# Attention with two mixture-of-experts layers in one kernel: scores by weight part, pages one per block, wide idle products in the opening, another order in the drain

## The chip, the cores and the metric

One core of a Trainium2 chip runs the kernel, with its five engines: TensorE (PE), VectorE (DVE), ScalarE (ACT), GpSimd (POOL) and SyncE (SP). The metric is the time of one execution on the device in microseconds (us); lower is better.

## What is computed

The inputs are q, k and v of shape (2 batches, 8 heads, 576 rows, 64 columns) in f32. Each row of the scores keeps its 32 largest values, and a softmax over these weighs the rows of v. The result goes through two mixture-of-experts layers with 8 experts each.

```python
scores = scale * np.matmul(q, k.transpose(0, 1, 3, 2))
kth = np.partition(scores, -top_k, axis=-1)[..., -top_k:-top_k + 1]
scores = np.where(scores >= kth, scores, -1000000000.0)
attn = np.exp(scores - np.max(scores, axis=-1, keepdims=True))
attn = attn / (np.sum(attn, axis=-1, keepdims=True) + 1e-09)
x = np.matmul(attn, v)                       # then (2 * 576, 8 * 64)
x = _moe_ref(x, ...)                         # argmax expert, capacity, relu(x @ w1) @ w2, times the gate
return _moe2_ref(x, ...)                     # the same without a capacity
```

## The kernel before, in words

The attention stage cuts the work into 8 units (2 heads of one batch each) and every unit into 9 blocks of 128 query rows: 4 per head, and one, the fifth in order (tile `None`), that holds the last 64 rows of both heads and so needs twice the products (the two-head tile). That makes 72 blocks, numbered 0 to 71, and 36 pairs. `seq` gives their order. One pass of the loop `for i in range(L)` deals with several blocks at once, each at another step, and the order in which the program issues instructions is written out by hand there:

- `scores(*seq[i + 4])`: TensorE multiplies q and k, both split into a high and a low f32r part that lie below each other, in two weight parts (four for the two-head tile). Columns 0 to 511 go to a score bank `sc` (a bank of its own for each of the two blocks of a pair, two pairs in flight), the last 64 columns to the end of `pt`. ScalarE copies both into `s` (lines 319).
- `folds` and `chain` on VectorE find the 32nd largest value: `folds` takes maxima and minima of quarters of a pair of blocks ("hi", line 338, is its first instruction and reads `sc` and `s` of both blocks), and each block's `chain` is four MAX8 and three MATCH_REPLACE8. `woven` puts a pair's two chains and the folds of the next pair into one order, from a string of letters.
- `limits` (GpSimd) makes the bounds of a finished pair; `lowered` (GpSimd, `shifted`) and `below` (ScalarE, a relu, `under`) then prepare a block, and `flip` on TensorE transposes `shifted` into `pt` and adds the transposed `under` as a large negative number, so that `expo` (ScalarE, `pT`) gives zero for all that is not kept.
- `value` multiplies `pT` with v and with ones and gates beside it; `value_out` copies the sums out.

Each unit's q, k and v are transposed some blocks ahead through one page buffer `pg`: six pages `turn`, one `turn_tails`, one `v_turn` (line 294, emptied by ScalarE at line 295) and one `v_gates` (line 301, emptied at 302). The table that `at(i, job, ...)` fills says in which block each runs: `turn` in blocks i0-12 to i0-7 ahead of the unit's first block i0, `turn_tails` in i0-6, `v_turn` in i0-3, `v_gates` in i0-2. The last two share their blocks with the first two `turn` of the next unit.

`begin` does the first unit's transposes and the first four blocks' scores. `spin` issues products of a constant tile with zeros, whose results nobody reads; `free` is a piece of 74 columns of the bank `xb`.

The last four blocks are the drain, with an order of their own (`drain`, `back_half`). The last block's kept scores come from VectorE: `first_shift` and `first_exp` take the exponent of all scores with the row's maximum off, and one instruction into `kept` multiplies by "not below the 32nd". Behind that stand the check counts (`missed`, `flags`), the last sums, and the gating of the first mixture-of-experts layer (line 1200 on), which also frees the loads of its weights.

## Time and profile before

| | |
|---|---|
| three timed runs | 631.38, 629.01, 631.46 us; median 631.38 |
| profiled execution | 631.72 us, its span 630.1 us |
| mean granted TensorE clock | 0.96 of full speed |
| busy TensorE / VectorE / ScalarE / GpSimd | 598.6 / 502.4 / 417.5 / 192.0 us |
| attention stage | to about 286 us |

The span is what the trace covers; the time also has what lies around it. Times in rows count from the span's start. PE is TensorE's products, PEld its loading of weights, which runs beside them; a product's row is longer than its distance to the next, since products overlap. "<-" names whom an engine waited for. The granted clock is 1.00 at 2.4 GHz and 0.50 at 1.2 GHz.

### The profile page before, as it was taken

The numbers are of one execution on the slowest core, as the hardware profiler recorded it, in microseconds if no ns is written. First come the engines' busy times: TensorE is split into PE (matmuls) and PEld (weight loads), VectorE is DVE, ScalarE is ACT, GpSimd is POOL, SyncE is SP. The second block draws the span as 40 slices with busy tenths as digits, with TensorE's granted clock in tenths as the row PEclk, the third lists the DMA queues.
The fourth block names the chain that finished last, engine by engine and source line by source line (L and its number), as shares of the span: only waits on it lengthen the run. The fifth ranks groups of instructions, "written<-read, shape, count | busy, mean of one in ns | idle before, by whom it ended". The sixth has DMA issues, their size and how long they took to land.

```text
span 630.1 us, 13986 instructions
## 1 busy us (share of the span) xinstructions
PE 598.6 (95%) x4839; PEld 556.4 (88%) x4839; DVE 502.4 (80%) x1728; ACT 417.5 (66%) x970; POOL 192.0 (30%) x422
## 2 busy tenths in 40 slices
PE   8899999999999999896999999999999999999995
PEld 6788989898989899785889999999999899999984
DVE  6868999999999999967677788785358797888740
ACT  5467878786878787641477777775246578787641
POOL 8356355645465334324201011100011312111010
PEclk7589999998999999986899999999999999999999
DMA  7610150416070000004797677677394976777650
GB/s 147 156 40 20 45 151 21 126 29 128 21 137 2 20 2 20 1 20 138 265 354 234 207 241 218 220 270 260 110 301 169 339 250 230 234 270 259 219 204 19
DMA packets 78640, 96.05 MB, mean 152 GB/s; under 512 B 33797, under 2 KB 40453, under 8 KB 78560
## 3 DMA queue, kind: packets, MB, share of 16 engines
q1 hardware_dynamic: 73632, 84.07, 43.0%
q0 software_dynamic: 3728, 10.70, 5.2%
q8 instruction: 41, 0.67, 0.4%
q10 hardware_dynamic: 1200, 0.30, 0.2%
q14 instruction: 39, 0.32, 0.2%
HBM read 82.32 MB, written 13.22 MB: 152 GB/s over the span
## 4 chain that ended last, share of the span: by engine, by line
PE 38%; DMA 8%; issue 4%; DVE 1%; ACT 0%; POOLq 0%; POOL 0%; ACTq 0%; DVEq 0%
PE pp L1041 8%; DMA out_dram<-yr,sidx 8%; PE pp L1080 7%; PE pp L1043 3%; PE pp L1082 3%; PE pp L1034 2%; PE pt L998 2%; PE pl L1094 1%; PE pp L1038 1%; PE pp L1037 1%; PE pp L1074 1%; PE pp L1039 1%; PE pp L1078 1%; PE pp L1076 1%; PE pp L1077 1%
## 5 line engine op out<-in xcount | busy, mean ns | idle before, releaser
L412 PE MATMUL xb<-vx,pT 128*128 128x73 f32 (+1 forms) x800 | 95.2, 269 | 0.0
L1041 PE MATMUL pp<-xT,w1c 128*128 128x416 f32 (+4 forms) x320 | 93.9, 361 | 0.5 <-DVE xT L1004 0.5
L412 PEld LDWEIGHTS xb<-vx,pT 128*128 128x128 f32 (+1 forms) x800 | 88.3, 183 | 2.3 <-issue 1.6
L969 DVE TENSOR_TENSOR w2c<-raw,w2c 128x512 fp32r<-128x512 f32 x112 | 74.2, 686 | 17.9 <-ACT w2c L968 17.8
L1080 PE MATMUL pp<-hT,w2c 128*128 128x416 f32 (+4 forms) x320 | 88.0, 353 | 0.0
L1082 PE MATMUL pp<-hT,w2c 128*128 128x208 f32 (+4 forms) x320 | 78.5, 245 | 0.0
L1043 PE MATMUL pp<-xT,w1c 128*128 128x208 f32 (+4 forms) x320 | 77.9, 243 | 0.0
L391 PE MATMUL pt<-ident,shifted 128*128 128x128 f32 x355 | 70.1, 283 | 3.6 <-ACT pT L400 2.1
L968 ACT ACTIVATE w2c<-raw 128x512 fp32r<-128x512 f32 x112 | 66.7, 623 | 7.8 <-SPq L1336 4.1
L969 DVE TENSOR_TENSOR w1c<-raw,w1c 128x512 fp32r<-128x512 f32 x96 | 60.8, 687 | 7.7 <-ACT w1c L968 7.4
L392 PE MATMUL pt<-negid,under 128*128 128x128 bf16 x355 | 66.0, 223 | 0.0
L1020 ACT ACTIVATE t<-pp 128x208 f32<-128x208 f32 (+4 forms) x120 | 37.6, 313 | 41.2 <-PE pp L1043 29.6
L1041 PEld LDWEIGHTS pp<-xT,w1c 128*128 128x128 f32 x320 | 60.1, 188 | 1.5 <-DVE xT L1004 0.9
L1082 PEld LDWEIGHTS pp<-hT,w2c 128*128 128x128 f32 x320 | 61.2, 191 | 0.0
L1043 PEld LDWEIGHTS pp<-xT,w1c 128*128 128x128 f32 x320 | 61.1, 191 | 0.0
L391 PEld LDWEIGHTS pt<-ident,shifted 128*128 128x128 f32 x355 | 51.0, 144 | 10.9 <-POOL lg L437 2.2
L1080 PEld LDWEIGHTS pp<-hT,w2c 128*128 128x128 f32 x320 | 60.2, 188 | 0.0
L356 DVE MAX8 top<-y 128x8 f32<-128x160 f32 x216 | 58.7, 312 | 0.0
L968 ACT ACTIVATE w1c<-raw 128x512 fp32r<-128x512 f32 x96 | 53.5, 621 | 7.2 <-SPq L1336 6.1
L319 ACT ACTIVATE s<-sc 128x512 f32<-128x512 f32 x72 | 43.0, 598 | 19.5 <-PE sc L318 17.5
L382 ACT ACTIVATE under<-s,nb 128x576 bf16<-128x576 f32 x71 | 54.2, 766 | 2.3 <-POOL nb L374 2.3
L385 POOL TENSOR_SCALAR shifted<-s,nb 128x576 f32<-128x576 f32 x71 | 53.2, 752 | 5.7 <-PE pt L392 1.6
(327 smaller groups left out, 1441.7 us busy)
## 6 DMA issues: line engine op xcount, KB each, us to landing
raw<-in_moe_w_dram SPq DMA_DIRECT2D x62, 1024.0 KB, 5.8
out_dram<-zero SPq DMA_DIRECT2D x3, 768.0 KB, 3.7
y<-yr POOLq DMA_DIRECT2D x8, 256.5 KB, 4.4
kraw<-in_k_dram SPq DMA_DIRECT2D x8, 256.0 KB, 3.1
vraw<-in_v_dram SPq DMA_DIRECT2D x16, 128.0 KB, 3.0
vx<-in_v_dram SPq DMA_DIRECT2D x16, 128.0 KB, 2.6
w2c<-in_moe_w_dram SPq DMA_DIRECT2D x4, 512.0 KB, 7.5
x<-xn SPq DMA_DIRECT2D x15, 128.0 KB, 1.8
```

The lines of the kernel that those rows point to most:

```text
L356: ops.append(lambda w=w, cur=cur: nc.vector.max(w, cur))
L382: nc.scalar.activation(under[k % 3][:, :S], s, AF.Relu, bias=nb[:, 1:2], scale=-BIG)
L385: nc.gpsimd.tensor_scalar(shifted[k % 3][:, :S], s, nb[:, 0:1], 1.0, op0=OP.add, op1=OP.mult)
L391: both = (nc.tensor.matmul(pt[:, o], shifted[k % 3][:, o], ident, is_transpose=True, start=True, stop=False), nc.tensor.matmul(pt[:, o], u ...
L392: nc.tensor.matmul(pt[:, o], under[k % 3][:, o], negid, start=False, stop=True))
L412: nc.tensor.matmul(o, pT[:, c2, cols], z["v"][:, c2, hh], start=(c2 == 0), stop=(c2 == NC - 1))
L968: nc.scalar.activation(o[:, 0], src_, AF.Copy)
L969: nc.vector.tensor_tensor(o[:, 1], src_, o[:, 0].bitcast(F32), op=OP.subtract)
L1041: nc.tensor.matmul(ph[:, :2 * n].rearrange("p (w n) -> p w n", w=2), w[f][:, 0, d], xT[:, d, :, :n], start=st, stop=False)
L1043: nc.tensor.matmul(ph[:, :n], w[f][:, 1, d], xT[:, d, 0, :n], start=False, stop=sp)
L1080: nc.tensor.matmul(py[:, :2 * n].rearrange("p (w n) -> p w n", w=2), w[f][:, 0, o], hT[:, f, :, :n], start=st, stop=False)
L1082: nc.tensor.matmul(py[:, :n], w[f][:, 1, o], hT[:, f, 0, :n], start=False, stop=sp)
```

## The change

1. `scores` goes through the weight parts one by one, and with each through both pieces of columns; before it did one piece with all parts, then the other. The second block's products no longer depend on the copy of the first block's scores.
2. `v_turn` and `v_gates` of units 2 to 7 run in blocks i0-5 and i0-4; unit 1's stay in blocks 6 and 7.
3. In the opening `wide_spin` (512 columns, read as twice the same 256) takes the place of most `spin`, in fewer products; in `begin` they write to the second bank of pair 1.
4. The drain is written anew: the values of block 67 and the flip of 68 come earlier, the chain of block 68 runs ahead of that of 69, `limits` of that pair is done by halves, and both last blocks (70 and 71) get the exponent by `apart` and the product by `keep` on VectorE.

The rest of the loop issues what it issued before.

```diff
-            kept = wk.tile([128, NC * 128], F32, name="kept", bufs=1)
-            nc.gpsimd.memset(kept[:, S:], 0.0)
+            kept = [wk.tile([128, NC * 128], F32, name=f"kept{i}", bufs=1) for i in range(2)]
...
+                z_ = pair(k_)
+                sc, s = z_.sc, z_.s
+                places_ = ((pt_[:, M * 128:S], slice(M * 128, S)), (sc[:, j_], slice(0, M * 128)))
+                for n_, (l, r) in enumerate(ops):
+                    for w_, (o, w) in enumerate(places_):
+                        m_ = nc.tensor.matmul(o, l, r[:, w], start=(n_ == 0), stop=(n_ == len(ops) - 1))
+                        if w_ and j_ and z_.read is not None:
+                            tc.declare_no_dep(m_.ins, z_.read.ins, reason="two banks")
+                for w_, (o, w) in enumerate(places_):
                     a_ = nc.scalar.activation(s[:, j_, w], o, AF.Copy)
...
+            def wide_spin(n, o):
+                for _ in range(n):
+                    nc.tensor.matmul(o.rearrange("p (a b) -> p a b", a=2), ones,
+                                     idle[:, None, :].to_broadcast([128, 2, 256]), start=True, stop=True)
...
-                spin(5, free)
+                pair(0)
+                wide_spin(2, pair(1).sc[:, 1])
...
-                spin(4, free)
+                wide_spin(3, pair(1).sc[:, 1])
...
-                spin(12, free)
+                wide_spin(4, pair(1).sc[:, 1])
...
-                    at(i0 - 3, v_turn, u)
-                    at(i0 - 2, v_gates, u)
+                    at(6 if u == 1 else i0 - 5, v_turn, u)
+                    at(7 if u == 1 else i0 - 4, v_gates, u)
...
-                if i < 5:
+                if i < 4:
+                    wide_spin((6, 6, 6, 3)[i], xb)
+                elif i == 4:
                     spin(12, free)
...
+            rest = bank()
+            a, b = chain(L - 4), chain(L - 3)
+            vec = woven((a, b), folds(K - 1, (0, 1)), "fafafafafbabafbabfabffb")
+            limits(K - 3)
+            relus = [fresh(L - 6), fresh(L - 5)]
+            run_jobs(L - 4, False)
+            do(vec[:17])
+            back(L - 7, lambda: do(relus))
+            back(L - 6)
+            run_jobs(L - 4, True)
+            run_jobs(L - 3, False)
+            do(vec[17:])
+            back(L - 5)
+            limits(K - 2, slice(0, 1))
+            relu = fresh(L - 4)
+            relu()
+            wide_spin(3, rest[:, 0])
+            value(L - 5)
+            value_out(L - 5)
+            pTs[L - 4] = expo(flip(L - 4))
+            run_jobs(L - 3, True)
+            limits(K - 2, slice(1, 2))
+            relu = fresh(L - 3)
+            run_jobs(L - 2, False)
+            a, b = chain(L - 2), chain(L - 1)
+            vec = woven((a, b), [], "ab" * 7)
+            do(vec[:2])
+            relu()
+            es = [apart(L - 2), apart(L - 1)]
+            do(vec[2:13])
+            keep(L - 2, es[0])
+            do(vec[13:])
+            keep(L - 1, es[1])
+            wide_spin(2, rest[:, 0])
+            back(L - 3)
...
+            wide_spin(2, rest[:, 0])
             value(L - 3)
             value_out(L - 3)
...
-            pTs[L - 2] = expo(flip(L - 2))
+            for c in range(NC):
+                o = slice(c * 128, c * 128 + 128)
+                nc.tensor.transpose(pt_[:, o], kept[0][:, o], ident)
+            pT = pTs[L - 2] = wk.tile([128, NC, 128], F32, name="pT")
+            nc.scalar.activation(pT.rearrange("p c s -> p (c s)"), pt_, AF.Copy)
```

Where instructions now stand, at three places. TensorE in the opening, behind the first unit's first three pages: of the small idle products the first is shown (`xb<-identr` are the tails' transposes, 64 columns). Before:

```order
L254 MATMUL sc<-identr,ks 128x128 x3
L479 LDWEIGHTS ones
L479 MATMUL xb<-idle,ones 128x74
...
L254 MATMUL xb<-identr,qs 128x64 [waits DVE_49]
L254 MATMUL xb<-identr,ks 128x64
```

And now:

```order
L255 MATMUL sc<-identr,ks 128x128 x3
L494 LDWEIGHTS ones
L494 MATMUL sc<-idle,ones 128x512 [waits Activation_49]
...
L255 MATMUL xb<-identr,qs 128x64 [waits DVE_49]
L255 MATMUL xb<-identr,ks 128x64
```

The wide products go to a score bank, and the first of them has a wait for ScalarE that the small ones had not.

TensorE in the blocks ahead of a unit (unit 2; `pg<-ident,vraw` is `v_turn`, `pg<-wgh` is `v_gates`, `pg<-identr` is `turn` of the unit after it). Before, in block i0-3:

```order
L412 MATMUL xb<-vx_144,pT 128x73 x5
L294 MATMUL pg<-ident,vraw 128x128 [waits DMAHW6_49,DMAHW5_49,PE_49]
L294 MATMUL pg<-ident,vraw 128x128 x3
L254 MATMUL pg<-identr,qs 128x128 [waits Activation_49]
L254 MATMUL pg<-identr,qs 128x128 x3
```

Now, in block i0-5:

```order
L423 MATMUL xb<-vx_146,pT 128x73 x4
L295 MATMUL pg<-ident,vraw 128x128 [waits DMAHW6_49,DMAHW5_49,PE_49]
L295 MATMUL pg<-ident,vraw 128x128 x3
L319 MATMUL pt<-qkT 128x64 [waits Activation_49]
L319 MATMUL sc<-qkT 128x512 [waits DVE_49]
```

The v page is followed by scores in place of another page, and the page behind it no longer waits for ScalarE at that point.

ScalarE in the drain (`pT` are exponents, `xl` the sums copied out, `under` the relus, `e` the exponents for the kept blocks). Before, from the exponents of blocks 66 and 67 on:

```order
L400 ACTIVATE pT<-pt 128x640 [waits PE_49,Activation_49] x2
L425 ACTIVATE xl_124<-xb 128x146 [waits PE_49]
L382 ACTIVATE under_139<-s,nb 128x576 [waits Pool_49]
L382 ACTIVATE under_131<-s,nb 128x576
L666 ACTIVATE e<-s,nb_4213 128x576 [waits Pool_49]
L400 ACTIVATE pT<-pt 128x640 [waits PE_49,Activation_49]
L425 ACTIVATE xl_124<-xb 64x146 [waits PE_49]
```

And now:

```order
L411 ACTIVATE pT<-pt 128x640 [waits PE_49,Activation_49] x2
L436 ACTIVATE xl_124<-xb 128x146 [waits PE_49]
L393 ACTIVATE under_141<-s,nb 128x576 [waits Pool_49]
L436 ACTIVATE xl_124<-xb 64x146 [waits PE_49]
L411 ACTIVATE pT<-pt 128x640 [waits PE_49,Activation_49]
L393 ACTIVATE under_133<-s,nb 128x576 [waits Pool_49]
L679 ACTIVATE e<-s,nb_4202 128x576 [waits Pool_49]
L679 ACTIVATE e<-s,nb_4206 128x576 [waits Pool_49]
```

The relu of block 69 (`under` behind the last `pT`) now stands behind the sums of block 67 and the exponent of 68, and both `e` stand behind that relu.

## Rows read from the trace of the kernel before

**Rows 1.** Busy time by stretches: length; each engine's busy us (x instructions); TensorE clock; DMA; GB/s.

```profile
9.20:9.50 0.30, 0.14 (x2) 0.02 (x1) 0.15 (x1) 0.30 (x1) 0.30 (x1) 0.80 0.62 46
10.00:20.00 10.00, 9.21 (x45) 7.61 (x45) 8.02 (x32) 4.31 (x13) 6.18 (x16) 0.50 0.65 149
36.00:38.00 2.00, 2.00 (x23) 1.82 (x21) 2.00 (x8) 1.28 (x5) 1.92 (x5) 0.83 0.00 0
60.00:80.00 20.00, 19.84 (x175) 18.06 (x174) 20.00 (x88) 16.74 (x38) 8.34 (x20) 1.00 0.19 60
272.00:274.00 2.00, 1.98 (x13) 1.48 (x14) 2.00 (x13) 1.54 (x3) 1.93 (x5) 0.55 0.23 65
```

**Rows 2.** Who waited for whom: VectorE in 0 to 170 us, TensorE in 62 to 262.

```profile
DVE hi L338 <- ACT s L319: 13.8, 11, 2.8
...
PE pg L254 <- ACT vT L295: 3.4, 5, 0.7
PE pg L254 <- ACT vx L302: 1.7, 5, 0.3
```

**Rows 3.** Timeline of VectorE, its "hi" instructions: start, length, in brackets the wait before.

```profile
18.07 0.46 DVE L338 TENSOR_TENSOR hi<-sc,s 128x288 f32<-128x288 f32 x1 [0.60 <-ACT s L319]
...
24.66 0.46 DVE L338 TENSOR_TENSOR hi<-sc,s 128x288 f32<-128x288 f32 x1 [1.44 <-ACT s L319]
...
34.38 0.46 DVE L338 TENSOR_TENSOR hi<-sc,s 128x288 f32<-128x288 f32 x1 [2.79 <-ACT s L319]
...
43.42 0.46 DVE L338 TENSOR_TENSOR hi<-sc,s 128x288 f32<-128x288 f32 x1 [2.10 <-ACT s L319]
...
59.57 0.46 DVE L338 TENSOR_TENSOR hi<-sc,s 128x288 f32<-128x288 f32 x1 [1.91 <-ACT s L319]
...
94.39 0.46 DVE L338 TENSOR_TENSOR hi<-sc,s 128x288 f32<-128x288 f32 x1 [0.29 <-ACT s L319]
...
123.10 0.46 DVE L338 TENSOR_TENSOR hi<-sc,s 128x288 f32<-128x288 f32 x1 [1.20 <-ACT s L319]
...
159.46 0.46 DVE L338 TENSOR_TENSOR hi<-sc,s 128x288 f32<-128x288 f32 x1 [1.36 <-ACT s L319]
```

**Rows 4.** Timeline of the opening: idle products on TensorE, and ScalarE's reading of the pages.

```profile
1.33 3.79 PE L479 MATMUL xb<-idle,ones 128*128 128x256 bf16 x17 [1.33 <-DVE idle L68]
...
6.27 1.05 ACT L504 ACTIVATE qkT<-sc 128x512 fp32r<-128x512 f32 x2
...
12.96 0.79 PEld L479 LDWEIGHTS <-ones 128*128 128x128 bf16 x12
12.96 0.96 PE L479 MATMUL xb<-idle,ones 128*128 128x74 bf16 x12
...
41.14 0.58 PE L479 MATMUL xb<-idle,ones 128*128 128x74 bf16 x12
```

**Rows 5.** Timeline of TensorE in the two blocks with two pages each, before unit 3.

```profile
112.27 0.55 PE L254 MATMUL pg<-identr,qs 128*128 128x128 f32 x4 [0.69 <-ACT vT L295]
...
116.96 0.54 PE L254 MATMUL pg<-identr,ks 128*128 128x128 f32 x4 [0.34 <-ACT vx L302]
```

**Rows 6.** Timeline of the drain: TensorE, ScalarE, VectorE, and the gating's first instruction.

```profile
269.29 1.29 PE L412 MATMUL xb<-vx,pT 128*128 128x73 f32 x10
...
272.02 0.34 PE L391 MATMUL pt<-ident,shifted 128*128 128x128 f32 x1 [1.45 <-POOL shifted L385]
...
272.73 0.78 ACT L666 ACTIVATE e<-s,nb 128x576 f32<-128x576 f32 x1
...
273.67 2.40 PE L412 MATMUL xb<-vx,pT 128*64 128x73 f32 x20
...
274.74 0.83 DVE L708 SCALAR_TENSOR_TENSOR kept<-s,top,e 128x576 f32<-128x576 f32 x1
...
282.21 2.35 PE L412 MATMUL xb<-vx,pT 128*128 128x73 f32 x20
...
285.81 0.24 DVE L1200 TENSOR_REDUCE mx<-lg 128x10 f32<-128x80 f32 x1 [0.33 <-DVEq L766]
```

## Prediction: what the change does to the time

> **What bounds the kernel now.** I read the page first, then busy time by stretches, then the waits, then the timeline of one VectorE instruction, and last the queues at the places that the edits touch. The profiled execution took 631.72 us over a span of 630.1, and the timed runs have a median of 631.38: a sum made against 631.72 stands 0.3 us above the median. All edits lie in the attention stage, which ends with the gating that starts at 285.81 us [rows 6]; the 344 us of mixture-of-experts stages behind it are not edited, and start when the gating is done.
>
> Between 60 and 80 us VectorE is busy for 20.00 of 20 us and TensorE for 19.84 [rows 1]: two engines side by side at their limit. VectorE's work on a pair of blocks begins with the instruction on "hi", so the starts of these are the clock of the stage. Where nothing is late they lie 6.8 to 7.0 us apart. What is late stands in brackets [rows 3], and it is always ScalarE's copy of the scores. In the first 170 us VectorE waits for that copy 13.8 us, 11 times [rows 2]. The change works at three places.
>
> First, the opening. The granted TensorE clock falls at 9.4 us, is 0.50 for the whole of 10 to 20 us, and comes back between 36 and 38 us [rows 1]. On that level TensorE's work takes longer: twelve small idle products 0.96 us against 0.58 at full clock [rows 4]. The waits at 18.07, 24.66 and 34.38 us, 0.60 + 1.44 + 2.79 = 4.83 us, lie in that stretch; those at 43.42 (2.10) and 59.57 (1.91) lie behind it, at full clock [rows 3].
>
> Second, the middle. From 62 to 262 us TensorE waits 3.4 + 1.7 us for ScalarE to empty the one page buffer [rows 2]. That happens where two pages stand in one block: the v page is followed at once by a q page, which waits 0.69 us, and in the next block the v gates by a k page, which waits 0.34 [rows 5]. These are the third and second block before a new unit, just ahead of the scores of the two-head tile, which have eight products where others have four. There VectorE waits 1.20 us at 123.10 and 0.29 at 94.39 [rows 3]; each of the two comes once more later, as the units alternate.
>
> Third, the drain. TensorE stands idle 1.45 us before 272.02, for the shifted block, and works from there to the last two values, which end at 284.56 (282.21 + 2.35) [rows 6], at first with a clock of 0.55 [rows 1].
>
> **The change part by part.** *Wide idle products.* The 5 + 4 + 12 small products around the first scores become 2 + 3 + 4 of 512 columns; the 12 in each of the first four blocks become 6, 6, 6 and 3. By the 17 products of 256 columns at the start, 3.79 us or 0.22 each [rows 4], a wide one takes 0.44 us at the low clock, and half, 0.22, at the full one (estimates). Against: the first two now go to the bank of pair 1, whose page ScalarE reads until 7.32 us (6.27 + 1.05) [rows 4]; the small ones ran at 6.4 us. The tails' transposes and all first scores are queued behind them and move back by 0.85 us. For: ahead of the fall at 9.4 us TensorE had transposes, small products and waits; now 5 wide products, 1.1 us of dense streaming, stand there, and 1.3 us more in each of the first blocks. I take it that the clock stays up through most of the opening. Then the three waits in the low stretch go, 4.83 us, less 0.85 for the late start: **-4.0 us**. Followed forward along ScalarE's copies, the "hi" of 24.66 comes at 22.5 (VectorE then no longer waits), that of 34.38 at 29.8 and that of 43.42 at 38.4, where most of its wait is left, which would be 4.6 to 5.0. I keep the lower number, since near 25 us TensorE still has a gap with eight transposes and a wait for ScalarE. Bounds: with the clock as low as before, 30 wide ones take 13.2 us for 5.5 (69 small ones at 0.08), 7.7 more, less 1.0 for a wait of the first pairs that the third edit removes: +6.7; at best -5.0.
>
> *Pages one per block.* For units 2 to 7 the v page moves from 3 to 5, and the v gates from 2 to 4 blocks before the unit, where no other page stands. Nothing is added: the same transposes, gate products and copies, no DMA, past no queue but TensorE's and ScalarE's own. The two waits, 0.69 + 0.34 = 1.03 us per unit, go [rows 5]. The scores of the two-head tile come 1.03 us earlier, which takes 1.03 of each 1.20 and all of each 0.29 [rows 3]: 2 x (1.03 + 0.29) = **-2.6 us**. Unit 1 keeps its places, so the wait at 59.57 stays. The 1.36 us at 159.46 [rows 3] follow a low-clock stretch, and I leave them. Bounds: 0, if TensorE is late at the two earlier blocks instead; -4.0 with these 1.36.
>
> *Scores by weight part.* The same products, and a dependency less: the second block of a pair no longer waits for the copy of the first. In the steady part I put nothing down: TensorE's instructions stay as many. VectorE hides them where it is the bound; where it waits they cost what they cost now. The Trainium skill, "TensorE: Matmul & The Clock Gate", section "Step-by-step: what each phase is for", says that weights may be loaded once and used by many products, which would save half the loads now that two products with the same weights stand together. The trace disagrees: twelve idle products with the same ones bring twelve loads [rows 4]. By the page's rule the rest of the two-head waits (0.3) and the 1.91 at 59.57 could go, and the sum would be 2.2 us lower.
>
> *The drain.* I follow TensorE's queue. The values of block 66 (of 0 to 71) end at 270.4 in both (269.29 + 1.1) [rows 6]. Then three wide products, 0.65, which fill the idle time of now; the twenty value products of block 67 at full clock, 2.2, to 273.25 (they stand behind the wait and the low clock now: from 273.67 on); the flip of block 68, 0.85 (1.65 from 272.02 to 273.67 at the low clock, half at the full one) to 274.1. Its exponent and the relu of block 69 follow on ScalarE, 0.7 to 0.8 each like "e" [rows 6], to 275.5. That is late next: the relu is queued behind both, and the flip of 69 waits for it. Flip 0.9, values 1.1, two wide 0.45, values 1.1: 279.05. The two exponents of the last pair are queued behind that relu and end near 277; VectorE's last chain stands still some 1.9 us for the first, and the two kept products, 0.83 each [rows 6], end at 278.2, before TensorE asks for them. Ten transposes 1.05, flags and two wide 0.5, the last values 2.35: 282.95 in place of 284.56, **-1.6 us**. VectorE's count and GpSimd's gate sums, which end with it now, move up as much. Removed are a shift on GpSimd, a relu, a flip; added a kept product, an exponent, five transposes. Bounds: 0, if the wait for the exponents holds up VectorE's flags and count; -2.8, if the relu is not late.
>
> Sum: 631.72 - 4.0 - 2.6 - 1.6 = **623.5 us**. About 0.5% (3.2 us) is what a measurement of this kernel can tell from no change.
>
> **The rivals.** *A, the clock drops within the opening.* For it: near 25 us TensorE has transposes and a wait, as before the fall at 9.4. A low stretch as at 272 [rows 1] lengthens six wide products by 1.3 and a pair of scores by 0.5, and the "hi" at 29.8 becomes 31.5; a second one doubles that. Opening -1.0: 626.5 us. The Trainium skill, the same page, section "Part 4: PE-mode transpose", says that transposes do not count as busy for the clock gate; by that rule A is likelier, as mostly transposes stand between the wide products. No row here separates the two. Against: the wide products follow in each of these blocks. Chance 0.25.
>
> *B, the clock rises no earlier than now.* Then the wide products are work at half speed on the engine that VectorE waits for: +6.7, and -4.2 from pages and drain: 634.2 us, slower than before. It is decided by the end of the first six wide ones, near 24 us: if the clock is 0.50 there, this is the case. For it: 20 us of scores and transposes at 0.50 [rows 1] did not bring the clock up. Against: they never streamed 2.6 us in one piece, as six wide ones do. Chance 0.10.
>
> *C, pages and drain give little.* VectorE and TensorE are both full [rows 1]: what the two-head tile gains can be lost at the blocks that now carry the pages, and in the drain the exponents behind the relu can delay flags and count; or the stage behind, whose start lies at a low clock, takes a part back. The opening's 4.0 and 0.6 of the rest: 627.1 us. Chance 0.15.
>
> **How the numbers follow.** Forecast 0.50 (623.5, own range 620 to 626), A 0.25, C 0.15, B 0.10. The best bounds together, -5.0 - 4.0 - 2.8, give 619.9, and the gating's own low clock can move all by 1 to 2 us. The range reaches to A and C and leaves B out: 618 to 630. Faster by over 0.5% (under 628.2) are nearly all of the forecast, three quarters of A, two thirds of C: 0.78. Within 0.5%, the rest of these and half of B: 0.15. Slower 0.07.
>
> **What would show it.** Right: a clock of 1.00 from 10 to 30 us; the "hi" of 34.38 near 30; brackets under 0.3 at the two-head pairs; TensorE's page waits near zero; a gating that starts near 277.5. Wrong: 0.50 still at 24 us, brackets above 2 us before 40, a 1.20 left in the middle, or a TensorE that waits for the kept blocks.

## The result, and the profile after

The changed kernel takes 622.72 us (median of four runs, 621.69 to 623.75), the kernel before 631.42 in the same comparison (629.01 to 634.45): a ratio of 0.986, interval 0.9814 to 0.9905, or 8.7 us less. The forecast was 623.5. The profiled execution took 622.74 us over a span of 621.1, at a mean clock of 0.98 (before: span 630.1, 0.96).

The total came out nearly as forecast, its parts did not. In the changed kernel "hi" is line 348, the scores line 319, the flip 402, the values 423, wide idle products 494. Four stretches make the span: to the ninth "hi", which ends the opening; from there to the last "hi"; from the last "hi" to the gating; and the stages behind.

| us | before | after | change | forecast |
|---|---|---|---|---|
| ninth hi starts | 66.43 | 61.61 | -4.82 | -4.0 |
| ninth to last hi (264.19, 253.50) | 197.76 | 191.89 | -5.87 | -2.6 |
| last hi to gating (285.81, 275.91) | 21.62 | 22.41 | +0.79 | -1.6 |
| gating to the span's end | 344.29 | 345.19 | +0.90 | 0 |

**The opening.** First the stretches of after, with the columns of [rows 1]; the stretches 9.20 and 10.00 stand there for before.

```profile
9.20:9.50 0.30, 0.30 (x2) 0.10 (x1) 0.07 (x1) 0.21 (x2) 0.23 (x1) 1.00 0.27 23
10.00:20.00 10.00, 9.10 (x55) 6.11 (x54) 9.26 (x37) 6.39 (x17) 6.29 (x15) 1.00 0.67 156
26.00:28.00 2.00, 2.00 (x9) 0.78 (x7) 2.00 (x11) 0.60 (x1) 0.42 (x3) 0.54 0.72 162
28.00:30.00 2.00, 2.00 (x11) 1.61 (x10) 0.72 (x4) 0.44 (x2) 1.23 (x4) 0.60 0.71 160
254.00:256.00 2.00, 0.25 (x2) 0.22 (x3) 2.00 (x8) 1.78 (x4) 1.84 (x5) 0.72 0.00 0
256.00:258.00 2.00, 2.00 (x13) 1.75 (x12) 2.00 (x11) 0.32 (x1) 0.82 (x3) 0.50 0.20 56
260.00:262.00 2.00, 2.00 (x15) 1.74 (x12) 1.97 (x12) 0.57 (x1) 1.31 (x3) 0.58 0.00 0
292.00:299.00 7.00, 6.57 (x36) 6.27 (x37) 3.63 (x8) 2.46 (x5) 0.94 (x1) 0.53 1.04 348
```

The clock no longer falls at 9.4 us; 10 to 20 us run at 1.00. A short low stretch (granted clock at 0.50) stands at 26 to 29.5, a long one in the drain (254.5 to 262), a short one behind the gating (282 to 285.5), and one over the first expert's products (292 to 299). The "hi" instructions of after, as in [rows 3]:

```profile
11.03 0.31 DVE L348 TENSOR_TENSOR hi<-sc,s 128x144 f32<-128x144 f32 x1 [0.23 <-ACT s L323]
...
16.75 0.44 DVE L348 TENSOR_TENSOR hi<-sc,s 128x288 f32<-128x288 f32 x1
21.80 0.44 DVE L348 TENSOR_TENSOR hi<-sc,s 128x288 f32<-128x288 f32 x1
30.41 0.46 DVE L348 TENSOR_TENSOR hi<-sc,s 128x288 f32<-128x288 f32 x1 [1.70 <-ACT s L323]
38.62 0.46 DVE L348 TENSOR_TENSOR hi<-sc,s 128x288 f32<-128x288 f32 x1 [1.27 <-ACT s L323]
...
54.76 0.46 DVE L348 TENSOR_TENSOR hi<-sc,s 128x288 f32<-128x288 f32 x1 [1.92 <-ACT s L323]
61.61 0.44 DVE L348 TENSOR_TENSOR hi<-sc,s 128x288 f32<-128x288 f32 x1
...
116.42 0.45 DVE L348 TENSOR_TENSOR hi<-sc,s 128x288 f32<-128x288 f32 x1
...
253.50 0.40 DVE L348 TENSOR_TENSOR hi<-sc,s 128x288 f32<-128x288 f32 x1
```

**The middle.** No bracket is left between 61.61 and 253.50. Of TensorE's waits in 62 to 252 us those for the page [rows 2] are gone, and one for the exponents has come, which costs nothing: VectorE is busy for 190.00 of these 190 us.

```profile
PE pt L319 <- ACT pT L411: 2.8, 5, 1.0
```

**The drain.** Its rows in the timeline of after (start, length, in brackets the wait), to set beside [rows 6]:

```profile
255.75 0.45 PE L402 MATMUL pt<-ident,shifted 128*128 128x128 f32 x1 [2.37 <-POOL lg L448]
...
262.52 0.81 PE L494 MATMUL sc<-idle,ones 128*128 128x512 bf16 x3
...
267.11 1.43 ACT L679 ACTIVATE e<-s,nb 128x576 f32<-128x576 f32 x2
...
267.91 0.82 DVE L684 SCALAR_TENSOR_TENSOR kept<-s,top,e 128x576 f32<-128x576 f32 x1 [4.05 <-ACT e L679]
...
275.91 0.24 DVE L1251 TENSOR_REDUCE mx<-lg 128x10 f32<-128x80 f32 x1 [0.33 <-POOL lg L791]
```

TensorE stands idle 2.37 us before the flip of block 66, as it did before the change (2.13 us, then without a fall):

```profile
266.42 0.30 PE L391 MATMUL pt<-ident,shifted 128*128 128x128 f32 x1 [2.13 <-ACT pT L400]
```

This time the clock falls there. Two flips and two sets of values, 255.75 to 262.52, take 6.77 us; all behind them is late, and VectorE waits 4.05 us for an exponent.

**Behind the gating.** The first expert's products begin in these rows, the upper one before the change, the lower one after it:

```profile
304.29 0.35 PE L1037 MATMUL pp<-xT,w1c 128*128 128x256 f32 x1 [0.19 <-issue]
```

```profile
291.95 0.35 PE L1088 MATMUL pp<-xT,w1c 128*128 128x256 f32 x1 [1.45 <-issue]
```

That is 18.48 and 16.04 us behind the gating, 2.4 us gained; from there to the span's end it is 325.81 and 329.15 us, 3.3 lost. In the changed kernel the clock is low from 292 to 299 us, over these products; before the change it was back by 303 us, ahead of them. How much of the 3.3 us this low stretch takes is not shown: after_again (below) has none there and still needs 327.65 us for that part.

### The profile page after: what moved, and what is told of

It is laid out like the page before. It is cut to its first block, busy times and chain, and to the rows that moved or that the text cites. A ratio compares the mean times of both kernels' runs of the same rounds, so it can differ in the third digit from the quotient of the medians.

```text
span 621.1 us, 13886 instructions
## 1 busy us (share of the span) xinstructions
PE 592.1 (95%) x4789; PEld 548.1 (88%) x4789; DVE 501.8 (81%) x1729; ACT 417.4 (67%) x970; POOL 191.5 (31%) x423
## 4 chain that ended last, share of the span: by engine, by line
PE 37%; DMA 8%; issue 5%; DVE 2%; ACT 1%; POOLq 0%; POOL 0%; ACTq 0%; DVEq 0%
DMA out_dram<-yr,sidx 8%; PE pp L1092 8%; PE pp L1131 7%; PE pp L1094 3%; PE pp L1133 3%; PE pp L1085 2%; PE pl L1145 1%; PE pp L1089 1%; PE pp L1088 1%; PE pt L1049 1%; PE pp L1090 1%; PE pp L1125 1%; PE pp L1127 1%; PE pp L1129 1%; PE pp L1128 1%
## 5 line engine op out<-in xcount | busy, mean ns | idle before, releaser
L402 PE MATMUL pt<-ident,shifted 128*128 128x128 f32 x350 | 68.5, 281 | 2.9 <-POOL lg L448 2.4
L403 PE MATMUL pt<-negid,under 128*128 128x128 bf16 x350 | 64.5, 222 | 0.3 <-ACT under L393 0.3
L319 PE MATMUL sc<-qkT 128*128 128x512 f32 x128 | 53.3, 482 | 0.0
```

Source lines behind the costliest of these rows:

```text
L319: m_ = nc.tensor.matmul(o, l, r[:, w], start=(n_ == 0), stop=(n_ == len(ops) - 1))
L402: both = (nc.tensor.matmul(pt[:, o], shifted[k % 3][:, o], ident, is_transpose=True, start=True, stop=False), nc.tensor.matmul(pt[:, o], u ...
L403: nc.tensor.matmul(pt[:, o], under[k % 3][:, o], negid, start=False, stop=True))
```

## The experiments

Ten altered kernels, and each of the two kernels once more, in three series: the first four of the table, the next four, the last four. Those of one series ran on one chip and share its runs of the kernel before (medians 630.38, 630.93 and 632.34); times are compared within a series. The four stretches of each profile, so that the parts can be told apart, then the median time and its ratio to the kernel before with the interval:

| us | ninth hi | ninth to last hi | last hi to gating | gating to end | median time | ratio |
|---|---|---|---|---|---|---|
| undo_pages | 61.62 | 197.90 | 24.41 | 344.5 | 626.26 | 0.9939 (0.9894 to 0.9985) |
| undo_scores | 62.94 | 191.91 | 21.19 | 340.9 | 620.55 | 0.9897 (0.9809 to 0.9985) |
| undo_spins | 61.78 | 191.90 | 21.22 | 342.1 | 620.44 | 0.9893 (0.9806 to 0.998) |
| undo_drain | 62.91 | 191.88 | 23.72 | 340.4 | 619.31 | 0.9863 (0.976 to 0.9966) |
| drain_fill | 64.10 | 191.91 | 19.62 | 340.1 | 615.06 | 0.9796 (0.975 to 0.9842) |
| open_fill | 59.90 | 191.89 | 22.42 | 341.2 | 617.98 | 0.9853 (0.9796 to 0.9909) |
| moe_fill | 60.09 | 191.88 | 22.52 | 339.7 | 621.15 | 0.9869 (0.9823 to 0.9915) |
| all_fill | 62.98 | 191.87 | 19.64 | 340.1 | 616.22 | 0.9821 (0.9766 to 0.9876) |
| undo_open | 64.74 | 191.90 | 22.80 | 347.0 | 626.93 | 0.9897 (0.9848 to 0.9946) |
| old_drain_fill | 62.94 | 191.91 | 20.04 | 344.9 | 622.54 | 0.9854 (0.9808 to 0.99) |
| after_again | 61.69 | 191.89 | 19.59 | 343.8 | 622.07 | 0.9843 (0.9794 to 0.9892) |
| before_again | 62.32 | 199.29 | 23.71 | 346.2 | 633.15 |  |

The second column is the same to 0.04 us wherever the pages are moved. The first and third differ from execution to execution even of one program, because the low stretches do. So a single profile prices the pages, but not an opening or a drain. The unaltered changed kernel stands in the last series only, and each of these intervals overlaps that of the change (0.9814 to 0.9905): by its time alone no kernel of the first two series is clearly told apart from the changed one. What the parts are worth is read from the stretches.

### undo_pages: the pages back in their old blocks

```diff
-                    at(6 if u == 1 else i0 - 5, v_turn, u)
-                    at(7 if u == 1 else i0 - 4, v_gates, u)
+                    at(i0 - 3, v_turn, u)
+                    at(i0 - 2, v_gates, u)
```

> The changed kernel (622.72 us) with the v page and the v gates back in blocks i0-3 and i0-2 for units 2 to 7; all else as changed. Theory 1, the pages made the gain of the middle by themselves: between 62 us and the last pair the waits of 0.29, 1.20, 0.57, 1.36, 1.20 and 0.29 return, about 4.9 us, the last pair's hi starts near 258.4 in place of 253.50, the time is 627 to 628. Theory 2, the pages made what the prediction put down for them: two waits of 1.2 and two of 0.3 return, 2.6 to 3.0 us, hi near 256.3, the time 625.3 to 625.7. Rival, the copies' and scores' new order made the middle's gain and the pages nothing: no bracket over 0.3 us returns, the time stays at 622.5 to 623.2.

Measured: 626.26 us, 5.7 to 7.0 us above the other three of its series. Its "hi" instructions:

```profile
61.62 0.44 DVE L348 TENSOR_TENSOR hi<-sc,s 128x288 f32<-128x288 f32 x1
...
89.58 0.46 DVE L348 TENSOR_TENSOR hi<-sc,s 128x288 f32<-128x288 f32 x1 [0.28 <-ACT s L323]
...
118.41 0.46 DVE L348 TENSOR_TENSOR hi<-sc,s 128x288 f32<-128x288 f32 x1 [1.32 <-ACT s L323]
...
153.23 0.46 DVE L348 TENSOR_TENSOR hi<-sc,s 128x288 f32<-128x288 f32 x1 [0.28 <-ACT s L323]
...
181.94 0.46 DVE L348 TENSOR_TENSOR hi<-sc,s 128x288 f32<-128x288 f32 x1 [1.20 <-ACT s L323]
...
210.09 0.46 DVE L348 TENSOR_TENSOR hi<-sc,s 128x288 f32<-128x288 f32 x1 [0.64 <-ACT s L323]
218.31 0.46 DVE L348 TENSOR_TENSOR hi<-sc,s 128x288 f32<-128x288 f32 x1 [1.28 <-ACT s L323]
...
259.52 0.39 DVE L348 TENSOR_TENSOR hi<-sc,s 128x288 f32<-128x288 f32 x1
```

The brackets sum to 5.0, and the stretch is 6.0 us longer than in all kernels with the pages moved. Theory 1 holds: the whole gain of the middle is the pages' (its time was put at 627 to 628). The last two pairs show how a page wait grows: in this execution the clock falls at 208 us, behind the wait of 0.34 us for the page at 207.57 (first TensorE's row, then the stretch behind it, with the clock third from the end),

```profile
207.57 0.54 PE L255 MATMUL pg<-identr,ks 128*128 128x128 f32 x4 [0.34 <-ACT vx L303]
```

```profile
208.00:209.00 1.00, 1.00 (x6) 0.91 (x5) 1.00 (x5) 0.72 (x2) 0.00 (x0) 0.55 0.00 0
```

and the unit then loses 0.64 + 1.28; the unit of 153.23, without a fall, loses one bracket of 0.28. In the kernel before the fall had come at 149 us, at that unit (0.57 and 1.36). Over the three profiles with the old pages the clock falls right behind 4 of the 15 second page waits between 62 and 252 us; over the eleven with the pages moved it is 1.00 there throughout.

### undo_scores: the old order of the scores

```diff
-                for n_, (l, r) in enumerate(ops):
-                    for w_, (o, w) in enumerate(places_):
-                        m_ = nc.tensor.matmul(o, l, r[:, w], start=(n_ == 0), stop=(n_ == len(ops) - 1))
...
+                for o, w in ((pt_[:, M * 128:S], slice(M * 128, S)), (sc[:, j_], slice(0, M * 128))):
+                    for n_, (l, r) in enumerate(ops):
+                        nc.tensor.matmul(o, l, r[:, w], start=(n_ == 0), stop=(n_ == len(ops) - 1))
+                    a_ = nc.scalar.activation(s[:, j_, w], o, AF.Copy)
```

> The changed kernel with the scores as they were: one piece of columns with all weight parts, its copy, then the other piece, and the second block's products waiting for the copy of the first. Theory as predicted: a cost of nothing in the steady part, time 622.4 to 623.4, no bracket over 0.3 us between 62 and 253 us. Rival: the surplus of the middle's gain over the forecast (5.87 measured against 2.6) is the missing dependency: waits of VectorE for the copy return at the two-head pairs, 2 to 3.3 us, time 624.7 to 626. If one load did for two products with the same weights, TensorE's busy time in the steady part would rise here by the loads that come back.

Measured: 620.55 us, under the 622.4 to 623.4 of the theory; no bracket in the middle. From 62 to 252 us TensorE is busy for 186.83 us here and 186.83 in the changed kernel, with 1688 and 1689 weight loads: no load was saved. The changed kernel's rows of the one-head scores in 60 to 255 us (count, then us in total and mean ns) show a load for every product:

```profile
L319 PE MATMUL pt<-qkT 128*128 128x64 f32 x100 | 23.6, 236 | 2.3 <-ACT pT L411 2.0
...
L319 PEld LDWEIGHTS pt<-qkT 128*128 128x128 f32 x100 | 19.0, 190 | 4.3 <-ACT pT L411 3.3
L319 PEld LDWEIGHTS sc<-qkT 128*128 128x128 f32 x100 | 18.9, 189 | 2.2
```

The Trainium skill, "TensorE: Matmul & The Clock Gate", section "Step-by-step: what each phase is for", has weights loaded once and used by many products. A program written as this one does not get that: in these rows 200 products bring 200 loads, though each pair has the same weights.

### undo_spins and undo_open: the opening

undo_spins puts the small idle products back; undo_open puts the old order of the scores back as well.

```diff
-                wide_spin(2, pair(1).sc[:, 1])
+                spin(5, free)
...
-                wide_spin(3, pair(1).sc[:, 1])
+                spin(4, free)
...
-                wide_spin(4, pair(1).sc[:, 1])
+                spin(12, free)
...
-                    wide_spin((6, 6, 6, 3)[i], xb)
+                    spin(12, free)
```

> The changed kernel with the small idle products (74 columns) back in the opening. Theory: the wide ones alone kept the granted clock up, so it falls near 9.4 us again and stays at 0.50 to beyond 30 us; the waits of 0.60, 1.44 and 2.79 us return, hi of pair 9 starts 4 to 5 us later than 61.61, and the time is 626.7 to 627.7. Rival: the new order of the scores or the missing dependency already shortens the opening, then the waits before 40 us add up to less than 3 us more than in the changed kernel and the time is 623 to 625.

> The changed kernel with both the small idle products and the old order of the scores in the opening and after it; pages and drain as changed. So far each of the two was put back alone, and in neither run did the clock fall at 9.4 us (hi of pair 9 at 61.78 and 62.94, 61.61 with both parts of the change). Theory 1, each alone closes the gap: the kernel before falls at 9.4 us because the second block's products wait 0.51 us for ScalarE's copy behind a stretch of small and idle work, the new order takes the wait away, the wide products fill what stands before it. Then with both put back the fall at 9 us returns in a part of the executions, as in the kernel before, whose times lie in two groups (623.8 to 627.2 at a mean clock of 0.966 to 0.976, 630.2 to 636.1 at 0.955 to 0.964): times here in two groups 5 to 6 us apart, about 618 to 621 and 624 to 627. Theory 2, something else of the change (pages, drain) keeps the opening at full clock: one group, 618 to 622, and hi of pair 9 at 61.5 to 64.

("Pair 9" in both is the ninth "hi".) The stretch from 9 to 19 us in undo_spins, in undo_scores and in undo_open, each kernel by itself:

```profile
9.00:19.00 10.00, 8.67 (x69) 6.33 (x69) 8.73 (x34) 7.05 (x17) 7.20 (x18) 1.00 0.69 153
```

```profile
9.00:19.00 10.00, 8.27 (x52) 5.89 (x51) 8.03 (x32) 6.69 (x17) 7.14 (x17) 1.00 0.68 148
```

```profile
9.00:19.00 10.00, 8.70 (x44) 7.30 (x44) 7.33 (x29) 5.12 (x13) 7.08 (x18) 0.53 0.68 153
```

With one of the two put back the clock stays up here, with both it falls at 9 us. Over all fourteen profiles, the three without either part (before, before_again, undo_open) have their first fall at 9, 12 and 9 us, the eleven with one or both of them none ahead of 23.5 us. The four runs of undo_spins (618.66 to 620.74 us) and of undo_scores (618.69 to 621.26) have mean clocks of 0.973 to 0.982. The six of undo_open lie at 0.963 to 0.967 in four executions (626.58 to 628.09) and at 0.973 and 0.979 in two (624.56, 622.57); its median is 4.9 us above that of after_again in the same series. Not all of that is the opening: against the profile of after_again, undo_open is longer by 3.0 us there, 3.2 in the drain and 3.1 behind the gating. My theory for undo_spins, that the wide products alone did it, fell; its 620.44 us lie under both ranges that I had given. Of theory 1 for undo_open the fall at 9 us came in the one profile there is; the two groups of times are less clear, and higher, than it had them. What the order takes away stands in TensorE's timeline, of undo_open:

```profile
9.03 0.34 PE L318 MATMUL pt<-qkT 128*128 128x64 f32 x2
9.88 1.22 PE L318 MATMUL sc<-qkT 128*128 128x512 f32 x2 [0.50 <-ACT s L319]
```

and of undo_spins, where the second block's products follow one another:

```profile
9.34 0.30 PE L319 MATMUL pt<-qkT 128*128 128x64 f32 x1
9.47 0.48 PE L319 MATMUL sc<-qkT 128*128 128x512 f32 x1
```

That this wait is what lets the clock fall is not shown. The same wait passed without a fall behind it in undo_scores, which has the wide products ahead of it, and in before_again, which has not (each by itself):

```profile
10.03 0.73 PE L318 MATMUL sc<-qkT 128*128 128x512 f32 x2 [0.50 <-ACT s L319]
```

```profile
9.69 0.73 PE L318 MATMUL sc<-qkT 128*128 128x512 f32 x2 [0.51 <-ACT s L319]
```

Nor was the order of the products put back without the dependency.

What the opening takes follows the number of low stretches in it. In the kernels with the wide products the ninth "hi" starts at 59.90 and 60.09 us without one, at 61.61 to 61.69 with one, at 62.91 to 62.98 with two and at 64.10 with three. undo_spins has two and 61.78, so no run shows that the wide products shorten the opening once the order is new. In eight of the fourteen profiles one of these stretches begins within 1.5 us of the same place: the second page wait (0.34 us) of unit 1, whose pages the change leaves in blocks 6 and 7. The eighth "hi" then waits 3.45 to 3.49 us in place of 1.9, as in undo_spins:

```profile
54.93 0.46 DVE L348 TENSOR_TENSOR hi<-sc,s 128x288 f32<-128x288 f32 x1 [3.46 <-ACT s L323]
```

### undo_drain, drain_fill and old_drain_fill: the drain

undo_drain has the old drain under all else of the change. drain_fill adds one line to the changed kernel, ahead of the flip that waits 2.37 us; old_drain_fill adds the same to undo_drain.

```diff
             back(L - 7, lambda: do(relus))
+            wide_spin(8, rest[:, 0])
             back(L - 6)
```

> The changed kernel with the drain as it was before. In the changed kernel the stretch from the last pair's hi to the gating takes 22.41 us, before 21.62. Theory 1, the new order is itself the worse one: the stretch takes 21.6 again and the gating starts near 275.1, the time is about 0.8 lower, 621.5 to 622.2. Theory 2, the new order is better by the 1.6 of the prediction, but a low clock from 255.4 to 261 us, which comes from the idle 2.37 us of TensorE ahead of it and not from the order, took 2.4 us: then the old order meets the same idle stretch at the same place of the program, its clock falls as well, and it takes 23 to 24.5 us, time 623.5 to 625. If the clock stays at 1.00 there with the old order, the two theories are not told apart by this run, and a fill of the idle stretch has to do it.

> The changed kernel with eight wide idle products (0.22 us each at full clock, 1.76 us) put on TensorE ahead of the flip of block 66, where it stood idle for 2.37 us. Theory: the low clock from 255.4 to 261 us comes from this idle stretch; it stays at 1.00, the two flips and two sets of values between 255.75 and 262.52 (6.77 us) take about 4.2, the exponents for the kept blocks come 2.4 us earlier, the wait of 4.05 us before the first kept product falls to about 1.7, the gating starts near 273.5, and the time is 620.0 to 620.8. Rival: what follows in the drain is bounded by ScalarE's or VectorE's order, not by TensorE: the low stretch goes and the gating moves by less than 1 us, time 621.8 to 622.7. Second rival: the clock falls all the same, later, and the time is 622.7 to 624.

> The changed kernel with the old drain, and eight wide idle products in it at the place of the filled kernel (ahead of the flip of block 66). With the new drain the fill took the stretch from the last pair's hi to the gating from 22.41 to 19.62 us. Theory, the new order is worth the 1.6 us of the prediction once the clock stays up: with the old order the stretch takes 21 to 21.6 us, and the time is 1.5 to 2 us above that of the filled new drain, 616.5 to 617.5. Rival, the old order is as good when the clock stays up (its own idle time of 1.45 us before the shifted block is what the low clock needs to begin): 19.5 to 20.2 us, time within 0.7 of 615.1. Third case, the clock falls later in the old order, at that idle time: 22 us or more.

The drain of drain_fill:

```profile
255.74 1.89 PE L494 MATMUL sc<-idle,ones 128*128 128x512 bf16 x8
258.27 0.30 PE L402 MATMUL pt<-ident,shifted 128*128 128x128 f32 x1 [0.64 <-POOL lg L448]
...
262.25 0.81 PE L494 MATMUL sc<-idle,ones 128*128 128x512 bf16 x3
...
267.63 0.82 DVE L684 SCALAR_TENSOR_TENSOR kept<-s,top,e 128x576 f32<-128x576 f32 x1 [1.25 <-ACT e L679]
...
275.63 0.24 DVE L1252 TENSOR_REDUCE mx<-lg 128x10 f32<-128x80 f32 x1 [0.33 <-POOL lg L792]
```

From the flip to the three idle products it is 3.98 us (258.27 to 262.25) in place of 6.77, the wait for the exponent is 1.25 in place of 4.05, and the stretch is 19.62 in place of 22.41. Over all profiles with the new order and no fill the clock fell in the drain in seven of eight, and the stretch took 21.2 to 24.4; in the one without a fall, after_again, it took 19.59. With the old order it fell in all three (21.62, 23.71, 23.72). With the fill it fell in none of three. So the order is priced at full clock, 20.04 for the old (one profile) and 19.59 to 19.64 for the new (three): 0.4 us. In old_drain_fill TensorE's wait of [rows 6] for the shifted block is still there, at the same 1.45 us, and brings no fall:

```profile
262.68 0.33 PE L400 MATMUL pt<-ident,shifted 128*128 128x128 f32 x1 [1.45 <-POOL shifted L394]
```

In time drain_fill is the lowest of all, 615.06 us (613.38 to 617.34). Its theory had 620.0 to 620.8: the drain's 2.8 us came as expected, and nothing here shows where the rest comes from. old_drain_fill's 622.54 and after_again's 622.07, of one series, are not told apart; by its stretch the rival was right, its time of within 0.7 us of 615.1 was not. undo_drain's 619.31 (615.64 to 622.31) lies below what either theory had and says nothing against the new order: its own drain took 23.72, as theory 2 had it, and its first expert ran without a low stretch.

### open_fill, moe_fill and all_fill

```diff
+                        if f == turn and a == (1, 1, 0):
+                            wide_spin(6, xb)
                         f(*a)
...
-                for q, n_ in zip(tiles_of(0), (10, 5)):
+                for q, n_ in zip(tiles_of(0), (10, 15)):
```

The first piece is open_fill, the second moe_fill; all_fill has both and the fill of the drain.

> The changed kernel with six wide idle products (1.32 us) put on TensorE between the two pages of block 2, where it stood idle for 1.76 us before 25.57. Theory: the low clock from 26 to 29.5 us comes from this gap; it stays at 1.00, the six wide products and the scores behind it (3.6 us at 25.94 to 29.55) take about 2.2, the hi at 30.41 loses its wait of 1.70 to about 0.3, and the waits behind it keep or lose a part: time 621.0 to 621.8. Rival: the clock stays up, but the time is taken back by the next pair's waits (1.27 at 38.62, 1.92 at 54.76), which grow: 622.3 to 623.

> The changed kernel with ten more idle products of 256 columns (0.11 us each at full clock) ahead of the first expert's products, where TensorE stood idle for 1.45 us before 291.95. In the changed kernel these products run at a clock of 0.50 to 0.58 from 292 to 299.3 us (0.21 us from one to the next, 0.12 behind it), in the kernel before at full clock. Theory: the low stretch comes from this gap, the lead of the first products (12.3 us) is then not taken back to 9.6: the time is 620.0 to 621. Rival: the experts wait for their weights from DRAM anyway (DMA share 1.04 from 290 to 300), and what the clock gives back is lost in waits for them: 622.3 to 623.

> All three fills in one kernel. Theory: the three low stretches are gone and their gains add up, 1.2 + 2.4 + 2.2: 616.5 to 618. Rival: moving one stretch moves the next to where its idle time is not filled, so that one or two low stretches come back elsewhere: 619 to 621.5.

Measured: 617.98 (615.48 to 623.12), 621.15 (615.88 to 623.94) and 616.22 us (612.99 to 620.17). The first is 3 us under what its theory had, the others within 0.3 us of theirs. In open_fill the clock stays at 1.00 to 253 us and the ninth "hi" starts at 59.90. But in moe_fill, whose opening is that of the changed kernel, it does so too (60.09): this gap brings a fall in some executions only, and two profiles don't price its fill. The same with moe_fill: the first expert runs at full clock there, and also in open_fill and drain_fill, which have no fill at that place. Both stay open. all_fill loses its opening to low stretches at 35 and 49 us, places without a fill, as its rival had it, and is no better than drain_fill. undo_scores and old_drain_fill, without the opening's fill, have the same two, so the fill is not shown to have moved them there.

### after_again and before_again

> The changed kernel once more, unaltered, beside the others. Theory, which low stretches an execution has differs from one execution to the next: the time lies in 616 to 624, the profile shows the low stretch of the drain again (TensorE idle for 2.4 us in every execution) and not necessarily those of 26 and 292 us; the ratio to the kernel before is 0.980 to 0.990. Rival, the low stretches of the first profile (26, 255, 282 and 292 us) belong to the program and all come back at the same places, time 622 to 624.

> The kernel before once more, for a second profile. Theory: its times lie in two groups because the clock falls at 9 us in some executions and not in the others. If this execution takes 624 to 627 us, the profile shows a clock of 1.00 from 10 to 24 us and the waits at hi of 0.60, 1.44 and 2.79 us are gone or small; if it takes 630 to 635, the stretch at 0.50 from 9 to 36 us is there again. Rival: the groups come from another place, then the opening is the same in both.

after_again: 618.61 to 624.79 us. Its low stretches are 26 to 29.5 and 275 to 285 us; those of 255 and 292 us are absent, although TensorE is idle for 2.36 us in the drain as ever:

```profile
255.81 0.30 PE L402 MATMUL pt<-ident,shifted 128*128 128x128 f32 x1 [2.36 <-POOL lg L448]
```

So the theory held but for the drain, which I had expected to fall each time. before_again took 633.15 us, and its opening is neither of the two that I had described:

```profile
9.00:12.00 3.00, 1.78 (x16) 1.39 (x14) 1.86 (x5) 2.55 (x7) 2.57 (x7) 1.00 0.60 104
12.00:19.00 7.00, 6.58 (x33) 5.45 (x32) 6.61 (x28) 2.56 (x7) 4.70 (x12) 0.51 0.70 168
19.00:25.00 6.00, 5.61 (x60) 4.71 (x58) 5.91 (x24) 3.85 (x9) 2.93 (x21) 1.00 0.63 141
25.00:32.00 7.00, 5.41 (x43) 4.79 (x44) 6.19 (x29) 4.44 (x10) 4.38 (x11) 0.56 0.71 156
```

It falls at 12 and at 25 us and is back in between; the ninth "hi" starts at 62.32, only 0.6 us later than after the change. This execution lost its time elsewhere: at two page waits with low stretches (145 and 210 us; 199.29 for the middle) and in the drain (264 to 275 us). Between these two profiles, of before_again and after_again, the change gains 0.6 in the opening, 7.4 in the middle, 4.1 in the drain and 2.4 behind it.

## Why the prediction's total was right, point by point

**Opening, -4.0: -4.82 in the first pair of profiles, not by the wide products alone.** Most steps held: clock 1.00 from 10 us on, though to 26 us and not to 30 as the sign had it, "hi" of 18.07 and 24.66 without a wait (16.75, 21.80), that of 34.38 at 30.41 and that of 43.42 at 38.62 with 1.27 of its wait left. Between the forecast's 29.8 and rival A's 31.5 lies 30.41, since one low stretch came, at 26 us: A's mechanism, at the gap that the prediction had named. A's price of 1.7 us nearly held too: the same "hi" starts at 28.71 in open_fill and 28.91 in moe_fill, without the stretch. So -4.82 is part luck: without that stretch, as in open_fill and moe_fill, the ninth "hi" comes 6.3 to 6.5 us earlier than in the first profile of before, more than the best bound of -5.0. Two steps failed. The late start of 0.85 did not come: first scores start at 8.43 in place of 8.20, and the first "hi" is at 11.03 in place of 11.73 (before_again: 11.09). And the cause that I gave, wide products alone, is not it: the small ones with the new order did as well, and so did the old order with the wide ones; with both undone it falls by 12 us in all three profiles. How much the opening gains depends on the execution of the kernel before that one compares with: 4.8 against the first profile, 0.6 against the second.

**Pages, -2.6: -5.87.** The mechanism was right, its size was not. The failed step is "the 1.36 us at 159.46 follow a low-clock stretch, and I leave them". Two things were left out. The unit of 151 to 159 us loses time by its pages as the others do (the bracket of 0.57 at 151.17 was not counted), and the low stretch there follows a page wait itself; undo_pages had one at 208 us. And brackets understate the loss: by the distance from one "hi" to the next, 6.83 where nothing is late, the five places lose 0.55, 1.29, 2.10, 1.28 and 0.54, together 5.76, of which 4.91 stand in brackets. Nor did any of the 1.20 stay, of which I had left 0.17 each.

**Scores, 0: 0** in the steady part, as the price was put, with a load per product as the row of before had shown. In the opening the new scores were one of the two parts that each kept the clock up, which I had put down to the other; whether by their order or by the missing dependency is open.

**Drain, -1.6: +0.79.** The failed step is the clock. I had compared an old drain whose low stretch fell late, at 272 us, with a new one at full clock. At equal clock the order gives 0.4. My count for the new one, 21.62 - 1.6 = 20.0 us, was close to the 19.6 measured wherever the clock stayed up; that it would stay up over an idle stretch of more than 2 us was not argued, and it did in one of eight. The exponents behind the relu were the late step, as said: VectorE waits 1.25 us for the first at full clock (1.9 forecast).

**Behind, 0: +0.9**, as 2.4 gained ahead of the first expert and 3.3 lost from there on, over a low stretch that is not there in every execution; its own share is open.

So the nearness of the sum is luck, the errors cancelled: 3.3 too little in the middle and 0.8 in the opening, 2.4 too much in the drain and 0.9 behind. Rival B is refuted by the clock of 1.00 at 24 us. Rival A's one low stretch came, but with more gained than its -1.0. Rival C had the drain right and the pages wrong. The three signs named for the middle (no 1.20 left, brackets under 0.3, page waits gone) all showed; the gating at 275.91 was earlier than the 277.5 forecast.

## What to carry to other kernels

Price a wait by the distance between repeats of the same instruction, not by its bracket, and count a low-clock stretch that follows a wait to that wait. Where TensorE stands idle ahead of work that others wait for, idle products that end before that work can start are worth a trial: here a stretch took 19.62 us with eight products of 512 columns in it and 22.41 without, but an execution without them also came to 19.59, and behind the old drain the same eight are not seen in the time. Before a part is priced by one profile, look at a second one of the same program.

## What the runs showed of the hardware

The granted clock of one and the same program falls at different places from one execution to the next. The kernel before fell at 9 us for 27 us, and in its second profile at 12 and 25 us for 7 us each. The same gap of 1.76 us before 25.6 us brought a fall in both profiles of the changed kernel, and none in undo_pages, undo_scores, moe_fill and old_drain_fill; an idle stretch of 2.36 us in the drain passed without one once, in after_again. The 38 runs of the kernel before in the three series lie between 623.83 and 636.09 us. The Trainium skill, "TensorE: Matmul & The Clock Gate", section "Part 1: The HAM clock gate", calls the ramp at a kernel's start variable from run to run. These profiles agree in that the same 17 idle products at the start take 3.29 to 3.79 us, though the clock is noted as 1.00 there; and they show that later falls vary too.
